# Attention with sinks and a window, then a SwiGLU block: the order of the first groups, the engine of the sink tables, and the path of groups 4 and 5

## The chip, the cores and the metric

The kernel runs on one core of a Trainium2 chip. A core has five engines with a queue of instructions each: TensorE (matrix products; the profile calls it PE, its weight loads PEld), VectorE (DVE), ScalarE (ACT), GpSimd (POOL) and SyncE (SP). Sixteen DMA engines move data between the chip's main memory and the on-chip memory; a transfer is issued from the queue of SyncE, ScalarE or GpSimd, and a transfer that changes float32 to bfloat16 on its way is issued from GpSimd in this kernel. The metric is the time on the device in microseconds (us).

## What is computed

Causal attention over a window of 128 positions plus the first 4 positions as sinks, for 4 batches of 8 heads with 768 positions of 64 elements; the result, as 3072 tokens of 512 elements, goes through a gated block (512 to 1536 to 512). In short:

```python
scores = scale * q @ k.T
keep = (pos_k < 4) | ((pos_q - pos_k >= 0) & (pos_q - pos_k < 128))
a = softmax(where(keep, scores, -1e9))
x = (a @ v) as [batch * position, head * dim]        # 3072 x 512
g = x @ w_gate                                       # 3072 x 1536
out = (g * sigmoid(g) * (x @ w_val)) @ w_out         # 3072 x 512
```

Inputs and outputs are float32; the kernel computes its products in bfloat16 with float32 sums.

## The kernel before

The tokens are split into 12 groups of 256 positions, three to a batch (`g = 3 * b + c`). The steps of a group, by the names of the functions:

- `load_rows` brings keys and queries of a group as bfloat16 rows, `load_nat` does so in token order; `load_v` brings its values.
- `step_T` transposes rows on TensorE, two pairs of heads at a time, and evicts the result from PSUM by ScalarE (keys) or VectorE (queries). `xbar` does the same from the `load_nat` layout by DMA transposes.
- `step_S` makes scores, exponentials (ScalarE) and masks (VectorE, put into `later`).
- `step_K` makes the scores of the sinks for groups that don't start a batch. It needs `ks`, the sink keys of the batch, made by `step_ks` together with `vsb`, the sink values.
- `step_PV` multiplies by the values and normalises; `step_X` transposes the result into `xT`, by TensorE for groups below `XB`, by DMA from there on.
- `gate` is one unit of the gated block (512 columns of gate and of value), `down` one of the output product. Tiles of the block hold `SIZES` tokens; the first three hold 256, then four of 512, then one of 256.

`later` holds VectorE work that is emitted behind the next matmuls; `flush` emits it. Every engine gets its instructions in the order of the program text below.

```python
NROW = 6
XB = 5
FCH = [2, 2, 4, 4]          # the weights of gate and value come in these chunks of 128 columns
...
stp = pool("stp", 2)
...
def load_rows(g, pairs=ALL, tensors=(0, 1)):
    ...
    for i in tensors:
        for w in range(2):
            nc.gpsimd.dma_start(x[64 * w:64 * (w + 1), i, pairs],
                                by_rows((k, q)[i], b, w, pairs, c * 256))
...
# loads at the start
PA, PB = slice(0, 2), slice(2, 4)
new_rows(0)
first = []
for i, eng in ((0, nc.sync), (1, nc.scalar)):
    st = stp.tile([P, 2, 4 * D], FP32, tag="st", name="st")
    for w in range(2):
        eng.dma_start(st[64 * w:64 * (w + 1)], by_rows((k, q)[i], 0, w, PA, 0))
    first.append(st)
nc.gpsimd.iota(tq, ...)
nc.gpsimd.iota(tk, ...)
load_rows(0, PB)
...
load_v(0)
nc.gpsimd.iota(th8, ...)
load_rows(1)
load_gate(0)
load_v(1)
load_gate(1)
load_gate(2)
load_rows(2)
load_v(2)
load_gate(3)
...
def step_T(g, i, p2, evict=None):
    ...
    for pp in range(2):
        p = 2 * p2 + pp
        for r in range(4):
            for w in range(2):
                h = slice(64 * w, 64 * (w + 1))
                nc.tensor.matmul(pt[h, pp, r:256:4], x[h, i, p, r * D:(r + 1) * D],
                                 ident[h, h], ...)
    ...                                    # one eviction, ScalarE or VectorE

def xbar(g):
    ...
    for j in range(2):
        for i in range(2):
            nc.sync.dma_start_transpose((kTs, qTs)[i][b][:, :, t0:t0 + P], nats[g][:, i, j])

def step_ks(b):
    ks = const.tile([P, NP2, KW], BF16, tag=f"ks{b}", name="ks")
    nc.gpsimd.memset(ks, 0.0)
    kss.append(ks)
    for h in range(2):
        r = slice(h * D, (h + 1) * D)
        nc.gpsimd.tensor_copy(out=ks[r, :, h * NS:(h + 1) * NS], in_=kTs[b][r, :, 0:NS])
    vsb = const.tile([P, H, D + 1], BF16, tag=f"vsb{b}", name="vsb")
    nc.gpsimd.tensor_tensor(vsb, vcf[:, b:b + 1].broadcast_to(...), diag_h..., op=ALU.mult)
    vsbs.append(vsb)

def step_K(g):
    ...
    for p in range(NP2):
        nc.tensor.matmul(ps[32 * p:32 * p + KW], kss[b][:, p], qTs[b][:, p, ...], ...)
    es_t[g] = espool.tile([P, 256], BF16, tag="es", name="es")
    nc.scalar.activation(es_t[g], ps, AF.Exp, scale=scale)

def step_X(g, j):
    ...
    if g >= XB:
        ...                                # nc.sync.dma_start_transpose(xTs[tb]..., xns[g, j])
        return
    ...                                    # four transposes by TensorE, one copy by VectorE
...
# the start
warm(10)                                   # ten matmuls on zeros
nc.vector.tensor_copy(out=rows[0][:, 0, PA], in_=first[0])
nc.vector.tensor_copy(out=rows[0][:, 1, PA], in_=first[1])
step_T(0, 0, 0, "a")
step_T(0, 1, 0, "v")
step_S(0, 0)
step_T(0, 0, 1, "v")
step_T(0, 1, 1, "v")
step_S(0, 1)
...
pro(*PVs(0))
flush()
pro(*Xs(0))
flush()
later.append(A(step_ks, 0))
for i in range(4):
    load_out(i)
load_rows(3)
load_v(3)

us = [(alone, 0, 0), g0[0], (alone, 0, 0), g0[1], (alone, 0, 0),
      g1[0], g1[1], g0[2], g1[2], g0[3], g1[3], g0[4], g1[4], g0[5], g1[5],
      *g2, *downs(0), *downs(1), *downs(2)]
weave(us, slots(                           # (unit, attention steps that go into it)
    (0, T(1)), ((1, 2), Ss(1)), (2, [K(1)]), ((3, 3, 4, 4), PVs(1)), (4, Xs(1)),
    ((8, 8, 9, 9), T(2)), ((10, 11), Ss(2)), (11, [K(2)]),
    ((12, 12, 13, 13), PVs(2)), (14, Xs(2)),
    (15, [L(A(load_rows, 4), A(load_v, 4))]),
    ((15, 16, 17, 18), T(3)), ((19, 20), Ss(3)),
    (20, [...loads of groups 5, 6 and 7...]),
    ((21, 21, 22, 22), PVs(3)), (23, Xs(3)),
    ((21, 22, 22, 23), T(4)), ((24, 25), Ss(4)), (25, [K(4)]),
    ((26, 26, 26, 26), PVs(4)), (26, Xs(4))))
...
weave(gates(3) + downs(3), slots(
    (0, [A(xbar, 6)]), (0, [L(A(load_nat, 8), A(load_v, 8))]),
    ((0, 0, 1, 1), T(5)), (4, [A(step_ks, 2)]), *pair(5, 6, 2), ...))
```

`T(g)` of a group that starts a batch also puts `step_ks` of its batch into `later`.

Of the kernel before, what the change touches and what calls it, by code (L numbers as in the profile page):

```python
# [7 lines left out]
FP32 = mybir.dt.float32  # L8
# [6 lines left out]
def kernel(  # L15
# [26 lines left out]
    SIZES = [256, 256, 256, 512, 512, 512, 512, 256]  # L42
    assert sum(SIZES) == NTOK and NG == 12
    OFF = [sum(SIZES[:i]) for i in range(len(SIZES))]
    NROW = 6
    XB = 5

    VS = 72
    FCH = [2, 2, 4, 4]
    FOF = [(i, f - sum(FCH[:i])) for i in range(len(FCH))  # L50
           for f in range(sum(FCH[:i]), sum(FCH[:i + 1]))]
    scale = 1.0 / float(D) ** 0.5
# [1 line left out]
    def pool(name, bufs, psum=False):  # L54
        if psum:
            return ctx.enter_context(
                tc.tile_pool(name=name, bufs=bufs, space=bass.MemoryType.PSUM))
        return ctx.enter_context(tc.tile_pool(name=name, bufs=bufs))
# [2 lines left out]
    wpool = pool("wpool", 1)  # L61
    rowp = pool("rowp", 3)
    natp = pool("natp", 3)
    stp = pool("stp", 2)
    vpool = pool("vpool", 1)
    kqtp = pool("kqtp", 2)
    epool = pool("epool", 2)
# [12 lines left out]
    def bank(shape, dtype, name):  # L80
        return psum.tile(shape, dtype, tag="b", name=name)
# [4 lines left out]
    def by_rows(src, b, w, pairs, t0):  # L86

        hs = slice(2 * pairs.start + w, 2 * pairs.stop, 2)
        return src[b, hs, t0:t0 + 256].rearrange("p (m r) d -> m p (r d)", r=4)
# [7 lines left out]
    def load_rows(g, pairs=ALL, tensors=(0, 1)):  # L97
        b, c = divmod(g, GC)
        x = rows[g] if g in rows else new_rows(g)
        for i in tensors:  # L100
            for w in range(2):
                nc.gpsimd.dma_start(  # L102
                    x[64 * w:64 * (w + 1), i, pairs],
                    by_rows((k, q)[i], b, w, pairs, c * 256))
# [12 lines left out]
    def load_v(g):  # L117
        b, c = divmod(g, GC)
        va = vpool.tile([P, 2, H, VS], BF16, tag=f"va{g}", name="va")
        nc.vector.memset(va[:, :, :, D:D + 1], 1.0)  # L120
        for j in range(2):
            t0 = c * 256 + j * P
            nc.gpsimd.dma_start(  # L123
                va[:, j, :, 0:D], v[b, :, t0:t0 + P].rearrange("h p d -> p h d"))
        vas[g] = va
# [3 lines left out]
    def load_gate(i):  # L129
        f0, n = sum(FCH[:i]) * P, FCH[i] * P  # L130
        for lst, w, nm in ((wgs, moe_w_gate, "wg"), (wvs, moe_w_val, "wv")):
            t = wpool.tile([P, DMC, n], BF16, tag=f"{nm}{i}", name=nm)
            nc.gpsimd.dma_start(
                t, w[:, f0:f0 + n].rearrange("(c p) f -> p c f", p=P))
            lst.append(t)
# [16 lines left out]
    lt8 = const.tile([P, H], FP32)  # L152
    sk = const.tile([P, 1], FP32)
    zero = const.tile([P, 512], BF16)
    vsbs, kss = [], []


    PA, PB = slice(0, 2), slice(2, 4)
    new_rows(0)
    first = []  # L160
    for i, eng in ((0, nc.sync), (1, nc.scalar)):
        st = stp.tile([P, 2, 4 * D], FP32, tag="st", name="st")
        for w in range(2):
            eng.dma_start(st[64 * w:64 * (w + 1)], by_rows((k, q)[i], 0, w, PA, 0))
        first.append(st)
    nc.gpsimd.iota(tq, [[1, P]], base=0, channel_multiplier=0,
                   allow_small_or_imprecise_dtypes=True)
    nc.gpsimd.iota(tk, [[0, 1]], base=0, channel_multiplier=1,
                   allow_small_or_imprecise_dtypes=True)
    load_rows(0, PB)  # L170
    nc.vector.memset(zero, 0.0)
    nc.vector.tensor_scalar(ident, tq, tk, None, op0=ALU.is_equal)
    load_v(0)
    nc.gpsimd.iota(th8, [[-32, NP2], [-NS, 2]], base=0, channel_multiplier=1,
                   allow_small_or_imprecise_dtypes=True)

    load_rows(1)
    load_gate(0)
    load_v(1)
    load_gate(1)  # L180
    load_gate(2)
    load_rows(2)
    load_v(2)
    load_gate(3)

    tq2 = tq.rearrange("p (o x) -> p o x", o=1).broadcast_to([P, 2, P])
    nc.vector.tensor_scalar(mask[:, :, 0:P], tq2, tk, None, op0=ALU.is_lt)
    nc.vector.tensor_scalar(mask[:, :, P:2 * P], tq2, tk, None, op0=ALU.is_ge)
# [2 lines left out]
    nc.vector.tensor_scalar(flat0[:, P:3 * P], flat[:, P:3 * P], sk, None, op0=ALU.max)  # L191
    nc.vector.tensor_copy(out=flat0[:, 3 * P:4 * P], in_=flat[:, 3 * P:4 * P])

    nc.vector.memset(vcf, 0.0)
    for p in range(NP2):
        for w in range(2):
            h = 2 * p + w
# [17 lines left out]
    def step_T(g, i, p2, evict=None):  # L215
        b, c = divmod(g, GC)
        new_T(b)
        x = rows[g]
        pt = bank([P, 2, 256], FP32, "pt")
# [5 lines that stand above are left out]
                    nc.tensor.matmul(  # L225
                        pt[h, pp, r:256:4], x[h, i, p, r * D:(r + 1) * D],
                        ident[h, h], start=True, stop=True, skip_group_check=True)
        dst = (kTs, qTs)[i][b][:, 2 * p2:2 * p2 + 2, c * 256:(c + 1) * 256]
        if (evict or ("a", "v")[i]) == "a":
            nc.scalar.copy(out=dst, in_=pt)  # L230
        else:
            nc.vector.tensor_copy(out=dst, in_=pt)  # L232
# [7 lines left out]
                nc.sync.dma_start_transpose(  # L240
                    (kTs, qTs)[i][b][:, :, t0:t0 + P], nats[g][:, i, j])

    KW = 32

    def step_ks(b):
        ks = const.tile([P, NP2, KW], BF16, tag=f"ks{b}", name="ks")
        nc.gpsimd.memset(ks, 0.0)
        kss.append(ks)
        for h in range(2):
            r = slice(h * D, (h + 1) * D)  # L250
            nc.gpsimd.tensor_copy(  # L251
                out=ks[r, :, h * NS:(h + 1) * NS], in_=kTs[b][r, :, 0:NS])
        vsb = const.tile([P, H, D + 1], BF16, tag=f"vsb{b}", name="vsb")
        nc.gpsimd.tensor_tensor(
            vsb,
            vcf[:, b:b + 1].broadcast_to([P, H, D + 1]),
            diag_h.rearrange("q (h o) -> q h o", o=1).broadcast_to([P, H, D + 1]),
            op=ALU.mult)
        vsbs.append(vsb)
# [32 lines left out]
    def step_K(g):  # L292
        b, c = divmod(g, GC)
        if c == 0:
            return
        ps = bank([P, 256], FP32, "pk")
        for p in range(NP2):
            nc.tensor.matmul(  # L298
                ps[32 * p:32 * p + KW], kss[b][:, p], qTs[b][:, p, c * 256:(c + 1) * 256],
                start=True, stop=True, skip_group_check=True)  # L300
        es_t[g] = espool.tile([P, 256], BF16, tag="es", name="es")
        nc.scalar.activation(es_t[g], ps, AF.Exp, scale=scale)
# [119 lines left out]
    def A(fn, *a):  # L422
        return lambda: fn(*a)

    def T(g):
        b, c = divmod(g, GC)
        def last():
            step_T(g, 1, 1)
            if c == 0:
                later.append(A(step_ks, b))  # L430
        return [A(step_T, g, 0, 0), A(step_T, g, 1, 0), A(step_T, g, 0, 1), last]

    def Ss(g):
        return [A(step_S, g, p2) for p2 in range(2)]
# [27 lines left out]
        return sl  # L462


    def warm(n):
        ps = bank([P, 512], FP32, "w")
        for _ in range(n):
            nc.tensor.matmul(ps, zero[:, 0:P], zero, start=True, stop=True,
                             skip_group_check=True)

    warm(10)
    nc.vector.tensor_copy(out=rows[0][:, 0, PA], in_=first[0])  # L472
    nc.vector.tensor_copy(out=rows[0][:, 1, PA], in_=first[1])
    step_T(0, 0, 0, "a")
    step_T(0, 1, 0, "v")
    step_S(0, 0)
    step_T(0, 0, 1, "v")
    step_T(0, 1, 1, "v")
    step_S(0, 1)

    nc.vector.tensor_scalar(lt8, th8, float(NS), None, op0=ALU.is_lt)
    nc.vector.scalar_tensor_tensor(diag_h, th8, 0.0, lt8, op0=ALU.is_ge, op1=ALU.mult)
    nc.vector.memset(vcf[:, :, D:D + 1], 1.0)
    flush()
    pro(*PVs(0))
    flush()
    pro(*Xs(0))
    flush()
    later.append(A(step_ks, 0))
    for i in range(4):  # L490
        load_out(i)
    load_rows(3)
    load_v(3)

    g0, g1, g2 = gates(0), gates(1), gates(2)
    us = [(alone, 0, 0), g0[0], (alone, 0, 0), g0[1], (alone, 0, 0),
          g1[0], g1[1], g0[2], g1[2], g0[3], g1[3], g0[4], g1[4], g0[5], g1[5],
          *g2, *downs(0), *downs(1), *downs(2)]
    loads = {}

    def L(*fs):
        def f():
            for x in fs:
                x()
        return f

    weave(us, slots(
        (0, T(1)), ((1, 2), Ss(1)), (2, [K(1)]), ((3, 3, 4, 4), PVs(1)), (4, Xs(1)),
        ((8, 8, 9, 9), T(2)), ((10, 11), Ss(2)), (11, [K(2)]),
        ((12, 12, 13, 13), PVs(2)), (14, Xs(2)),  # L510
        (15, [L(A(load_rows, 4), A(load_v, 4))]),
        ((15, 16, 17, 18), T(3)), ((19, 20), Ss(3)),
        (20, [L(A(load_rows, 5), A(load_v, 5), A(load_nat, 6), A(load_v, 6),
                A(load_nat, 7), A(load_v, 7))]),
        ((21, 21, 22, 22), PVs(3)), (23, Xs(3)),
        ((21, 22, 22, 23), T(4)), ((24, 25), Ss(4)), (25, [K(4)]),
        ((26, 26, 26, 26), PVs(4)), (26, Xs(4))))

    def pair(ga, gb, sh=0):
        s = sh  # L520
# [4 lines left out]
                ((14, 14) if s else (13, 14), Xs(gb))]  # L525

    weave(gates(3) + downs(3), slots(
        (0, [A(xbar, 6)]), (0, [L(A(load_nat, 8), A(load_v, 8))]),
        ((0, 0, 1, 1), T(5)), (4, [A(step_ks, 2)]), *pair(5, 6, 2),
        (8, [A(xbar, 7)]), (9, [L(A(load_nat, 9), A(load_v, 9))]),  # L530
        (14, [A(xbar, 8)]), (14, [L(A(load_nat, 10), A(load_v, 10))])))
    weave(gates(4) + downs(4), slots(
# [42 lines left out]
```

## Time and profile before

| | |
|---|---|
| time, median of 3 runs | 284.14 us (283.5 to 286.56) |
| span of the profiled execution | 284.4 us, TensorE's clock 0.934 of full on average |
| TensorE matmuls | 250.3 us busy (88%), 2148 |
| VectorE | 165.4 us (58%), 336 |
| ScalarE | 110.6 us (39%), 213 |
| GpSimd | 73.6 us (26%), 107 |
| chain of work that ended last | TensorE 74%, DMA 9%, GpSimd 5%, VectorE 5% |
| read from main memory, written | 28.34 MB, 6.29 MB |

A line of the profile's tables names the line of the kernel (L298), the engine, and what is written from what (`pk<-qT,ks`). Names of tiles that the text uses: `st` staging tiles of group 0 in float32, `rows` and `nat` keys and queries as loaded, `pt` their transposes in PSUM, `s` and `e` scores and exponentials, `pk` and `es` the same for the sinks, `o` and `xn` attention output, `xT` its transpose, `wg`, `wv`, `wo` the weights, `pg`, `pv`, `pd` their products, `ks` and `vsb` the sink tables, `va` values. In the page's slices each digit stands for a fortieth of the span, 7.11 us, and gives a busy share in tenths.

### The profile page before, as it was taken

Reading aid. Unit: us, or ns where it says so; the run is one execution under the profiler, and the core shown is the slowest. Engines: PE = TensorE matmul, PEld = TensorE weight load, DVE = VectorE, ACT = ScalarE, POOL = GpSimd, SP = SyncE. Lnnn points to the kernel's source line nnn. Section 1 sums busy time; section 2 is a strip of 40 time slices with the busy share of each in tenths; the row PEclk is TensorE's granted clock in tenths of the full one; section 3 lists DMA queues with packets and bytes.
Section 4 is the critical chain, followed back from the end, with each engine's and each line's share of the span. In section 5 each row is a group of like instructions: output and inputs, shape, how many; then the busy total and the mean of one; then the engine's idle time right before and its main releaser. Section 6 shows DMA issues by size and latency. Waiting matters only on the chain.

```text
span 284.4 us, 5371 instructions
## 1 busy us (share of the span) xinstructions
PE 250.3 (88%) x2148; PEld 145.8 (51%) x2174; DVE 165.4 (58%) x336; ACT 110.6 (39%) x213; POOL 73.6 (26%) x107
## 2 busy tenths in 40 slices
PE   6785027999799999999999999978999999999995
PEld 1563015787587545545454454533445544558543
DVE  3566005478857626589851989503899329987400
ACT  1526000237146236474714655123565156233221
POOL 8964465000009990263500080000000000000000
PEclk9659557799999999999999999997999999999999
DMA  8999999100008999399935896157001130010022
GB/s 131 161 191 191 205 203 174 13 0 2 0 3 91 170 179 193 92 111 97 135 52 128 150 103 68 37 128 168 1 20 21 55 129 2 4 36 0 35 79 110
DMA packets 86792, 26.07 MB, mean 92 GB/s; under 512 B 71792, under 2 KB 83824, under 8 KB 86768
## 3 DMA queue, kind: packets, MB, share of 16 engines
q0 software_dynamic: 61760, 13.90, 54.4%
q1 hardware_dynamic: 24720, 11.57, 17.2%
q8 instruction: 17, 0.28, 0.4%
q10 hardware_dynamic: 288, 0.26, 0.3%
q14 instruction: 7, 0.06, 0.1%
HBM read 28.34 MB, written 6.29 MB: 122 GB/s over the span
## 4 chain that ended last, share of the span: by engine, by line
PE 74%; DMA 9%; POOL 5%; DVE 5%; issue 2%; SPq 2%; ACT 2%; POOLq 0%; DVEq 0%
PE pv L374 22%; PE pg L374 21%; PE pd L405 19%; PE o L322 4%; DMA wv<-in_moe_w_val_dram 4%; DMA wo<-in_moe_w_out_dram 4%; PE s L276 3%; PE pt L225 3%; POOL rows L102 2%; SPq L240 2%; DVE ht L388 2%; POOL va L123 2%; DVE xn L328 2%; ACT e L283 1%; DMA xT<-xn 1%
## 5 line engine op out<-in xcount | busy, mean ns | idle before, releaser
L374 PE MATMUL pg<-xT,wg 128*128 128x256 bf16 (+1 forms) x380 | 77.2, 336 | 5.3 <-DMA xT<-xn 2.9
L387 DVE SCALAR_TENSOR_TENSOR u<-th,pg 128x512 bf16<-128x512 f32 x72 | 49.2, 684 | 53.6 <-ACT th L381 53.2
L381 ACT ACTIVATE th<-pg 128x512 f32<-128x512 f32 x72 | 43.4, 603 | 86.4 <-PE pg L374 85.9
L374 PE MATMUL pv<-xT,wv 128*128 128x256 bf16 (+1 forms) x373 | 75.4, 332 | 0.9 <-DVE ht L388 0.5
L405 PE MATMUL pd<-wo,ht 128*128 128x512 bf16 (+1 forms) x289 | 65.7, 370 | 0.6 <-issue 0.2
L388 DVE TENSOR_TENSOR ht<-u,pv 128x512 bf16<-128x512 bf16 x72 | 49.5, 688 | 13.7 <-PE pv L374 6.9
L374 PEld LDWEIGHTS <-wg 128*128 128x128 bf16 x384 | 38.3, 101 | 32.3 <-DMA xT<-xn 3.1
L283 ACT ACTIVATE e<-s 128x512 bf16<-128x512 f32 (+1 forms) x96 | 46.0, 576 | 4.3 <-PE s L276 4.2
L374 PEld LDWEIGHTS <-wv 128*128 128x128 bf16 x384 | 34.9, 100 | 21.9 <-issue 3.2
L405 PEld LDWEIGHTS <-ht 128*128 128x128 bf16 x300 | 27.5, 98 | 27.2 <-issue 0.3
L409 ACT ACTIVATE ot<-pd 128x512 f32<-128x512 f32 (+1 forms) x25 | 14.5, 582 | 49.2 <-PE pd L405 43.9
L288 DVE TENSOR_TENSOR e<-e,mask 128x1024 bf16<-128x1024 bf16 (+1 forms) x48 | 29.1, 641 | 5.4 <-ACT e L283 5.2
L123 POOL DMA_DIRECT2D va<-in_v_dram x24 | 21.8, 936 | 3.7 <-issue 2.1
L322 PEld LDWEIGHTS <-e 128*128 128x128 bf16 x352 | 17.9, 102 | 7.8 <-DVE e L288 1.5
L328 DVE TENSOR_TENSOR xn<-o,rcp 128x256 bf16<-128x256 f32 x48 | 20.4, 424 | 1.7
L251 POOL COPY ks<-kT 64x16 bf16<-64x16 bf16 x8 | 1.6, 194 | 73.9 <-ACT kT L230 37.7
L322 PE MATMUL o<-va,e 128*128 128x65 bf16 x352 | 19.7, 200 | 0.7 <-DVE e L288 0.7
L225 PE MATMUL pt<-ident,rows 64*64 64x64 bf16 x384 | 16.0, 268 | 1.4 <-DVE rows L472 1.4
L225 PEld LDWEIGHTS <-rows 64*64 64x64 bf16 x384 | 13.4, 147 | 6.6 <-issue 4.1
L298 PE MATMUL pk<-qT,ks 128*32 128x256 bf16 x32 | 2.5, 297 | 16.0 <-POOL ks L251 16.0
L276 PE MATMUL s<-qT,kT 64*128 64x128 bf16 (+1 forms) x256 | 14.8, 248 | 1.6 <-DVE qT L232 1.6
L232 DVE CAST qT<-pt 128x512 bf16<-128x512 f32 x12 | 8.3, 692 | 10.5 <-PE pt L225 10.5
(44 smaller groups left out, 117.6 us busy)
## 6 DMA issues: line engine op xcount, KB each, us to landing
out_dram<-ot SPq DMA_DIRECT2D x23, 256.0 KB
va<-in_v_dram POOLq DMA_DIRECT2D x24, 128.0 KB, 6.1
wo<-in_moe_w_out_dram POOLq DMA_DIRECT2D x4, 384.0 KB, 12.2
nat<-in_k_dram POOLq DMA_DIRECT2D x12, 128.0 KB, 4.6
nat<-in_q_dram POOLq DMA_DIRECT2D x12, 128.0 KB, 5.3
rows<-in_k_dram POOLq DMA_DIRECT2D x10, 128.0 KB, 5.7
rows<-in_q_dram POOLq DMA_DIRECT2D x10, 128.0 KB, 5.5
wg<-in_moe_w_gate_dram POOLq DMA_DIRECT2D x2, 512.0 KB, 9.7
```

Of the source, the lines that this page charges most:

```text
L123: nc.gpsimd.dma_start(va[:, j, :, 0:D], v[b, :, t0:t0 + P].rearrange("h p d -> p h d"))
L225: nc.tensor.matmul(pt[h, pp, r:256:4], x[h, i, p, r * D:(r + 1) * D], ident[h, h], start=True, stop=True, skip_group_check=True)
L276: nc.tensor.matmul(pss[2 * pp + h][:, col:col + n], kTs[b][r, p, kk:kk + P], qTs[b][r, p, qq:qq + n], start=True, stop=True)
L283: nc.scalar.activation(e_t[g][:, h0 + h, lo:512], pss[2 * pp + h][:, lo:512], AF.Exp, scale=scale)
L288: nc.vector.tensor_tensor(e, e, m[:, :, lo:512].broadcast_to([P, 2, 512 - lo]), op=ALU.mult)
L322: nc.tensor.matmul(o, l, r, start=(i == 0), stop=(i == len(mms) - 1), skip_group_check=True)
L328: nc.vector.tensor_tensor(xns[g, j][:, 256 * hh:256 * (hh + 1)].rearrange("p (h d) -> p h d", h=4), po[:, :, 0:D], rcp.broadcast_to([P, 4, ...
L374: nc.tensor.matmul(ps[:, i * n:(i + 1) * n], ws[fi][:, c, fo * P:(fo + 1) * P], x[:, c], start=(c == 0), stop=(c == DMC - 1))
L381: nc.scalar.activation(th, pg, AF.Tanh, scale=0.5)
L387: nc.vector.scalar_tensor_tensor(u, th, 1.0, pg, op0=ALU.add, op1=ALU.mult)
L388: nc.vector.tensor_tensor(hts[tb][:, f:f + two].rearrange("p a n -> p (a n)"), u, pv, op=ALU.mult)
L405: nc.tensor.matmul(po, hts[tb][:, f, ts * P:(ts + 1) * P], wos[f // n][:, f % n, lo:hi], start=(f == 0), stop=(f == DFC - 1))
```

## The change

Four things are changed.

- **Group 0 pair by pair.** Keys and queries of the first two pairs of heads come in one float32 transfer each and are cast by VectorE and ScalarE; the other two pairs come by casting transfers from GpSimd's queue. Each pair is transposed, scored and masked by itself, with a few matmuls on zeros between, so that work can start when the first pair is there.
- **Group 1 earlier.** Its rows are the first thing loaded after group 0, and it is transposed and half scored before the values of group 0 are multiplied. The weights of gate and value come in five chunks instead of four, and the output weights are loaded ahead of the rows of group 3 in the starting block.
- **Sink tables by VectorE.** The copies of the sink keys and the product for the sink values leave GpSimd, whose queue also issues the loads. The key tables of all batches are one tile, cleared once at the start.
- **Groups 4 and 5 by the DMA crossbar.** Their keys and queries are loaded in token order and transposed by DMA, which the kernel does for the later groups already; with `XB = 4` so is the attention output of group 4. The steps of groups 1 to 6 move to other units accordingly.

```diff
-    XB = 5
+    XB = 4
-    FCH = [2, 2, 4, 4]
+    FCH = [2, 2, 2, 2, 4]
-    stp = pool("stp", 2)
+    stp = pool("stp", 4)
@@ loads at the start
-    for i, eng in ((0, nc.sync), (1, nc.scalar)):
-        st = stp.tile([P, 2, 4 * D], FP32, tag="st", name="st")
-        for w in range(2):
-            eng.dma_start(st[64 * w:64 * (w + 1)], by_rows((k, q)[i], 0, w, PA, 0))
-        first.append(st)
+    first = {}
+    for p in range(2):
+        for i, eng in ((0, nc.sync), (1, nc.scalar)):
+            st = stp.tile([P, 4 * D], FP32, tag="st", name="st")
+            eng.dma_start(st, by_pair((k, q)[i], p))
+            first[p, i] = st
+    nc.scalar.activation(warmed, one, AF.Exp)
+    pair_by_cast(2, 0)
     nc.gpsimd.iota(tq, ...)
     nc.gpsimd.iota(tk, ...)
-    load_rows(0, PB)
+    pair_by_cast(2, 1)
+    pair_by_cast(3, 0)
+    pair_by_cast(3, 1)
+    load_rows(1)
     load_v(0)
+    load_gate(0)
+    load_v(1)
     nc.gpsimd.iota(th8, ...)
-    load_rows(1)
-    load_gate(0)
-    load_v(1)
     load_gate(1)
     load_gate(2)
+    load_gate(3)
     load_rows(2)
     load_v(2)
-    load_gate(3)
+    load_gate(4)
+    for i in range(4):
+        load_out(i)
@@ step_ks
-        nc.gpsimd.memset(ks, 0.0)
-            nc.gpsimd.tensor_copy(
-                out=ks[r, :, h * NS:(h + 1) * NS], in_=kTs[b][r, :, 0:NS])
-        nc.gpsimd.tensor_tensor(
+            nc.vector.tensor_copy(
+                out=kss[r, b, :, h * NS:(h + 1) * NS], in_=kTs[b][r, :, 0:NS])
+        nc.vector.tensor_tensor(
             vsb, ...
@@ the start
-    warm(10)
-    ...
+    fill(8, bank([P, 512], FP32, "w"))
+    for p in range(2):
+        nc.vector.tensor_copy(out=rows[0][:, 0, p], in_=first[p, 0])
+        nc.scalar.copy(out=rows[0][:, 1, p], in_=first[p, 1])
+        pair_T(p, "a")
+    pair_S(0, 1)
+    pair_T(2, "v")
+    pair_S(1)
+    pair_mask(0)
+    pair_T(3, "v")
+    pair_S(2, 1)
+    pair_mask(1)
+    pair_S(3, 1)
+    pair_mask(2)
+    step_T(1, 0, 0, "a")
+    pair_mask(3)
+    step_T(1, 1, 0, "v")
+    step_T(1, 0, 1, "a")
+    step_T(1, 1, 1, "v")
+    step_S(1, 0)
+    masks1 = list(later)
+    later.clear()
+    step_PV(0, 0, 0)
+    step_PV(0, 0, 1)
+    flush()
+    step_PV(0, 1, 0)
+    step_PV(0, 1, 1)
+    step_X(0, 0)
+    flush()
+    step_S(1, 1)
+    step_X(0, 1)
+    ...
+    for m in masks1[:2]:
+        m()
+    step_ks(0)
+    for m in masks1[2:]:
+        m()
+    step_K(1)
     load_rows(3)
     load_v(3)
@@ the first units
-    us = [(alone, 0, 0), g0[0], (alone, 0, 0), g0[1], (alone, 0, 0),
-          g1[0], g1[1], g0[2], ...
+    us = [g0[0], (alone, 0, 0), g0[1], g1[0], g1[1], g0[2], ...
-        (0, T(1)), ((1, 2), Ss(1)), (2, [K(1)]), ((3, 3, 4, 4), PVs(1)), (4, Xs(1)),
-        ((8, 8, 9, 9), T(2)), ((10, 11), Ss(2)), (11, [K(2)]),
-        ((12, 12, 13, 13), PVs(2)), (14, Xs(2)),
-        (15, [L(A(load_rows, 4), A(load_v, 4))]),
-        ((15, 16, 17, 18), T(3)), ((19, 20), Ss(3)),
-        ...
-        ((21, 22, 22, 23), T(4)), ((24, 25), Ss(4)), (25, [K(4)]),
-        ((26, 26, 26, 26), PVs(4)), (26, Xs(4))))
+        (1, PVs(1) + Xs(1)),
+        ((5, 5, 6, 6), T(2)), ((7, 8), Ss(2)), (8, [K(2)]),
+        ((9, 9, 10, 10), PVs(2)), (11, Xs(2)),
+        (12, [...load_nat and load_v of groups 4, 5 and 6...]),
+        ((13, 14, 15, 16), T(3)), ((17, 18), Ss(3)), (18, [A(step_ks, 1)]),
+        (18, [A(xbar, 4)]),
+        ((19, 19, 20, 20), PVs(3)), (21, Xs(3)),
+        ((20, 21), Ss(4)), (21, [K(4)]), (22, [A(xbar, 5)]),
+        ((22, 22, 23, 23), PVs(4)), (23, Xs(4))))
@@ the first tile of 512 tokens
-        (0, [A(xbar, 6)]), (0, [L(A(load_nat, 8), A(load_v, 8))]),
-        ((0, 0, 1, 1), T(5)), (4, [A(step_ks, 2)]), *pair(5, 6, 2),
+        (0, [L(A(load_nat, 7), A(load_v, 7))]), (2, [A(xbar, 6)]),
+        (2, [L(A(load_nat, 8), A(load_v, 8))]), (5, [A(step_ks, 2)]), *pair(5, 6),
```

## The prediction

> **What bounds the kernel now.** I read four views in this order: the page's 40 slices (7.11 us each), the stretches of time around what they show, the chain of work that ended last, and the waits of TensorE. The slices first:
>
> ```profile
> PE   6785027999799999999999999978999999999995
> PEclk9659557799999999999999999997999999999999
> DMA  8999999100008999399935896157001130010022
> ```
>
> From slice 7 on TensorE is busy nine tenths at full clock, so most of the kernel is bound by TensorE. The exception is the front: slices 4 and 5 (28 to 43 us) are nearly empty, and the clock is at half before and after. By stretches (length, then busy us of each engine, clock, DMA share):
>
> ```profile
> core 0: us, PE busy (x) PEld busy (x) DVE busy (x) ACT busy (x) POOL busy (x), PEclk, DMA share, GB/s
> 0.00:25.00 25.00, 19.43 (x226) 12.82 (x226) 12.83 (x38) 8.36 (x17) 18.77 (x32) 0.73 1.30 167
> 25.00:41.00 16.00, 0.01 (x2) 0.01 (x3) 2.76 (x5) 2.48 (x6) 8.67 (x14) 0.64 1.39 199
> 41.00:53.40 12.40, 10.49 (x81) 7.43 (x82) 4.88 (x13) 1.58 (x3) 5.54 (x8) 0.64 1.32 131
> 53.40:284.40 231.00, 220.33 (x1843) 125.51 (x1867) 144.89 (x281) 98.18 (x189) 40.61 (x53) 0.99 0.58 74
> ```
>
> So 16.0 us pass with no matmul, 12.4 us follow at a clock of 0.64, and 231.0 us are nearly full. The waits of TensorE between 20 and 60 us name one cause, and the chain (start, duration, what) says what stood before it:
>
> ```profile
> PE pk L298 <- POOL ks L251: 16.0, 1, 16.0
> ```
>
> ```profile
> 13.78 11.86 DMA wv<-in_moe_w_val_dram
> ...
> 26.65 10.52 DMA wo<-in_moe_w_out_dram
> ...
> 38.18 0.91 POOL va L123
> ...
> 40.22 0.22 POOL ks L247
> ...
> 40.99 0.40 PE pk L298 x3
> 41.40 1.82 PE pg L374 x8
> ```
>
> TensorE wants the sink keys `ks` of batch 0 for the sink scores of group 1. GpSimd makes them, but only behind the loads that it issues earlier in program order: the output weights, the rows of group 3, the values of group 3. It holds at most eight loads open (the load issued at 16.33 starts right after the eighth before it landed, at 16.05), so its queue moves at the pace of the DMA, which is full until about 50 us. The two copies take 0.43 us; 16 us is the queue. The weights are no reason: the trace's completions put gate/value chunk 0 at 14.2 and 16.1 us, chunk 1 at 19.1 and 20.4, the last value weights at 35.2, the last output weights at 42.8.
>
> **What the skill says.** (1) "TensorE: Matmul & The Clock Gate", section "Part 1: The HAM clock gate", says that the array runs at half clock after an idle window of about 3.4 us and at full clock only after a sustained busy one. The trace agrees: eight 256-column matmuls take 1.86 us at 50 us and advance every 0.87 us from 53.5 us. (2) The same page, section "Architectural detail", says that VectorE, ScalarE and GpSimd are strictly first in, first out. The 16 us behind loads show that for GpSimd, and it means that table work put on VectorE makes everything behind it wait for its inputs. (3) "GPSIMD Engine Reference", section "Performance versus the Vector engine", measures a two-input elementwise operation 1.96 times slower on GpSimd. Here the `vsb` product (128x520) takes 1.06 us on GpSimd; with that ratio my estimate for VectorE is 0.54 us, no run of this kernel shows it.
>
> **The change part by part.**
>
> *Sink tables.* Two copies and one product leave GpSimd for VectorE, four times. At 2 x 0.2 for the copies (what they take on GpSimd) plus 0.54, that is 0.9 us a batch, 3.8 us in all. VectorE is busy 144.9 of 231 us in the long stretch, so three of the four are hidden. The first is in the front, and the wait of 16.0 us goes.
>
> *The front.* I lay it out anew. The first K and Q pair now comes in one transfer each. Before, all four staging transfers had landed at 6.55, after about 0.72 MB since 2.1 us; the first pair is half of the staging data, so about 4.5 us. Then:
> - pair casts to about 5.0, four pairs of transposes (16 matmuls; 32 took 1.08 to 1.92), scores, evictions and filler: about 1.7 us a pair at half clock, to about 11.5 us;
> - transposes of group 1: its rows land by about 10 us (same bytes ahead of them as before, when they landed at 12.3), 64 matmuls took 3.6 us cold: about 14.5;
> - scores of half of group 1 (0.62 to 0.8): 15.3; values of group 0 (4 steps): about 17, the values having landed near 12;
> - four normalisations on VectorE (0.18 + 0.42 each, 2.4 us), their transposes and two 0.42 copies, with the other half of the scores beneath: about 19.6;
> - VectorE: two tiny table operations (0.35), two masks (2 x 0.69), the key copies (2 x 0.2): about 21.7. Here the sink scores of group 1 wait some 2 us, in place of the 16;
> - first gate unit, two groups of eight matmuls at 0.87 us: 23.5. Values and normalisation of group 1, which VectorE sets (two masks 1.3, the unit's two products 1.4, normalisation 2.4, copies), to about 27.6; then two units of 1.74: 31.1 us.
>
> This is the point that the old kernel reaches at 53.4. Part of this comes from the old 41 to 53 us, which ran mostly cold. I add 1.4 us for cold windows in mine: **32.5**, a gain of **20.9 us** (18 to 23). Can the weights keep up? Bytes and order up to each chunk are nearly as before, so chunk 2 lands near 23, chunk 3 near 26, chunk 4 at 35.2. Chunk 4 is first read after five more units (8.7), the transposes (2.2) and half the scores of group 2: 44 us. The output weights (42.8) are needed past 65. All of it is in time.
>
> *Groups 4 and 5 by the crossbar.* These lines of TensorE's timeline (start, busy, operation) price what goes:
>
> ```profile
> 77.72 1.05 PE L374 MATMUL pg<-xT,wg 128*128 128x256 bf16 x8 [1.45 <-DVE xT L354]
> 94.38 0.63 PE L225 MATMUL pt<-ident,rows 64*64 64x64 bf16 x16
> 94.95 1.25 PE L405 MATMUL pd<-wo,ht 128*128 128x512 bf16 x5
> 116.11 1.08 PE L225 MATMUL pt<-ident,rows 64*64 64x64 bf16 x32
> 117.12 1.04 PE L374 MATMUL pv<-xT,wv 128*128 128x512 bf16 x3
> ```
>
> One transposing step holds TensorE for 0.57 us (94.38 to 94.95), two for 1.01 (116.11 to 117.12). Group 4: 4 x 0.57 = 2.3; group 5: 2 x 1.01 = 2.0; together **4.3 us**, all on the path, since TensorE has no idle there. Transposing the attention output of group 4 by DMA as well saves 2 x 0.22 = **0.4 us** (113.58 to 113.80). VectorE and ScalarE lose four evictions each of about 0.6, hidden. The DMA does it behind: the row loads of groups 4 to 6 are no longer held behind the tables on GpSimd's queue, so they can be on the chip long before; a DMA transpose holds its queue 1.2 us.
>
> *Reordering.* Group 2 finishes a unit earlier, so the wait of 1.45 us for its transposed output (first line above) should vanish: **-1.4 us**.
>
> *A new wait.* Group 4's output transposes stand behind group 5's four key/query transposes on one queue (4 x 1.3 = 5.2 us). These start about 0.9 us into the fourth of the six `down` units (2.6 to 3.5 us each), once the third's output is copied. The last output transpose then issues at about +7.8 us and lands 2.45 later (as the one before 193.28): +10.3, while TensorE gets there at +9.6. **+1.0 us** with some margin.
>
> Sum: 20.9 + 4.3 + 0.4 + 1.4 - 1.0 = 26.0. 284.1 - 26.0 = **258 us**.
>
> **The rivals.**
> 1. *The DMA takes the place of the tables.* For it: the DMA is saturated for the first 50 us, and the chain shows 11.86 and 10.52 us of weight loads. Against it: those are links only because GpSimd's queue ran through them; the completions are ahead of the need by 5 to 20 us. If an early unit did wait for weights, I lose 3 to 6 us: about 263.
> 2. *VectorE takes the place of GpSimd.* Tables on a strict queue: if batch 2's keys come late (four transposes issued three units before they are read), VectorE stops and TensorE after it. For: the margin is some 3 us by the queue count above. Against: in the old run the DMA queue ran well ahead of TensorE (the keys of group 9 were transposed from 158.3, their unit starts near 172). Cost if so 2 to 5 us: 260 to 263.
> 3. *The front stays cold and serial.* Pair by pair, each piece is a short chain TensorE, ScalarE/VectorE, TensorE. If no window fills, everything to the third unit runs at half clock: 36 instead of 32.5, and 261 to 262.
> 4. *The gain is hidden*: the time freed in front is lost again later. Against: after 53.4 TensorE is 95% busy (220.3 of 231.0), and nothing there waits for a fixed clock time. The one later wait of size, at 190 us (2.87 us for a transposed output, then a half-clock window), stays as it is.
>
> **Range and chances.** The front is worth 18 to 23, the crossbar 3 to 6, new waits 0 to 5. That gives 252 to 265. The 16 us wait has one clear cause, and the change moves its work away, so a gain under 2% (5.7 us) would need two rivals together: faster 0.96, same 0.02, slower 0.02.
>
> **What would show it.** Right: no wait of TensorE for `ks` over 3 us; first gate unit near 22 and the fourth near 32 us; the empty slices gone and clock 1.0 from about slice 4; no transposes by TensorE for groups 4 and 5; a wait of about 1 us for a transposed output where the 512-token tiles begin. Wrong: waits of early units for `wg` or `wv`; VectorE idle on transposed keys; a half-clock stretch past 30 us; a new wait over 3 us at the first 512-token tile.

## The result and the profile after

The changed kernel takes 273.8 us (median of 4 runs, 272.8 to 274.6) where the kernel before takes 285.4 in the same runs: a ratio of 0.960, 95% interval 0.952 to 0.968. The prediction was 258 us, with a range from 252 to 265. The direction was right, the size was not: 26 us were expected, and 11.6 came.

The slices of the page of the changed kernel (6.79 us each) show where to look:

```profile
PE   5039679999999958999999999969999999999995
PEclk9999999999999997999999999988999999999999
DMA  3949999999995379999149910462010320000122
```

The two empty slices at 28 to 43 us are gone. In their place slice 1 is empty and slice 2 three tenths busy, between 6.8 and 20 us, and the DMA, which used to be full from slice 0 on, is now weak in slices 0 and 2. Slices 14 and 15 (95 to 109 us) are thinner than before. The stretches around these places (length, busy us of each engine, clock, DMA share):

```profile
core 0: us, PE busy (x) PEld busy (x) DVE busy (x) ACT busy (x) POOL busy (x), PEclk, DMA share, GB/s
0.00:13.10 13.10, 3.60 (x8) 1.04 (x8) 3.03 (x15) 1.89 (x3) 6.37 (x14) 1.00 0.65 82
13.10:18.50 5.40, 1.08 (x18) 0.84 (x18) 0.72 (x2) 0.78 (x2) 0.92 (x1) 1.00 0.46 58
18.50:41.90 23.40, 19.03 (x283) 13.83 (x284) 17.32 (x46) 11.17 (x23) 17.79 (x25) 1.00 1.44 163
41.90:98.90 57.00, 55.76 (x622) 39.64 (x624) 40.20 (x83) 25.41 (x50) 25.84 (x31) 1.00 1.56 149
98.90:106.20 7.30, 3.34 (x18) 1.32 (x19) 0.69 (x1) 2.04 (x4) 4.45 (x6) 0.77 1.51 168
```

The clock of 1.00 in the first rows is not what the matmuls show. The trace has no entry of the clock before 24.3 us, and until then sixteen transposing matmuls take 1.06 us, while from 24.6 us on sixty-four take 1.97:

```profile
13.12 1.06 PE L486 MATMUL pt<-ident,rows 64*64 64x64 bf16 x16 [8.30 <-DVE rows L517]
24.65 1.97 PE L244 MATMUL pt<-ident,rows 64*64 64x64 bf16 x64
```

So TensorE ran at half clock up to there. In the first 13.1 us it does nothing but its 3.6 us of filler. DMA moves 82 and then 58 GB/s, where the kernel before had 167 GB/s over its first 25 us. The longest waits of TensorE in the changed kernel (waited for: us in total, times, longest) give the causes their names:

```profile
PE pt L486 <- DVE rows L517: 12.6, 2, 8.3
PE pg L388 <- DMA xT<-xn: 6.5, 2, 4.0
PE pk L312 <- DVE kss L265: 2.3, 1, 2.3
```

The 16.0 us for the sink keys have become 2.3. New are 12.6 us for the first two pairs of group 0, and 6.5 us for transposed outputs, of which the 4.0 at 98.9 us are new and the 2.5 at 178 us were there before (2.9 at 190 us). The front of the chain of work, with start and duration, says what the first of these is:

```profile
0.74 0.71 SPq L175
1.51 16.60 DMA st<-in_k_dram
18.14 0.30 DVE rows L517
18.48 1.06 PE pt L486 x9
```

The staging transfer of the second key pair, issued at 1.51, is read at 18.1 us. It brings 128 KB.

### The profile page after: what moved, and what is told of

It is laid out like the page before. It is cut to its first block, busy times and chain, and to the rows that moved or that the text cites. A ratio compares the mean times of both kernels' runs of the same rounds, so it can differ in the third digit from the quotient of the medians.

```text
span 271.5 us, 5112 instructions
## 1 busy us (share of the span) xinstructions
PE 240.5 (89%) x2016; PEld 138.4 (51%) x2039; DVE 165.6 (61%) x347; ACT 109.8 (40%) x213; POOL 71.1 (26%) x93
## 4 chain that ended last, share of the span: by engine, by line
PE 74%; DVE 9%; DMA 9%; SPq 3%; ACT 3%; issue 2%; DVEq 0%; ACTq 0%
PE pv L388 22%; PE pg L388 21%; PE pd L419 19%; DMA st<-in_k_dram 6%; PE o L336 4%; PE s L290 4%; DMA xT<-xn 2%; DVE ht L402 2%; DVE xn L342 2%; SPq L259 2%; PE pt L244 2%; ACT e L297 1%; DVE e L302 1%; DVE u L401 1%; PE pt L486 1%
## 5 line engine op out<-in xcount | busy, mean ns | idle before, releaser
L388 PE MATMUL pg<-xT,wg 128*128 128x256 bf16 (+1 forms) x380 | 75.3, 329 | 6.7 <-DMA xT<-xn 6.5
L388 PE MATMUL pv<-xT,wv 128*128 128x256 bf16 (+1 forms) x374 | 74.9, 328 | 1.4 <-DVE ht L402 0.8
L388 PEld LDWEIGHTS <-wg 128*128 128x128 bf16 x384 | 37.6, 99 | 33.0 <-issue 6.1
L388 PEld LDWEIGHTS <-wv 128*128 128x128 bf16 x384 | 34.5, 98 | 21.5 <-issue 4.0
L297 ACT ACTIVATE e<-s 128x512 bf16<-128x512 f32 (+1 forms) x88 | 42.9, 580 | 3.6 <-PE s L290 3.5
L111 POOL DMA_DIRECT2D nat<-in_k_dram x16 | 14.2, 903 | 55.5 <-DMA qT<-nat 50.9
L302 DVE TENSOR_TENSOR e<-e,mask 128x1024 bf16<-128x1024 bf16 (+1 forms) x44 | 26.9, 649 | 2.9 <-ACT e L297 2.9
L336 PEld LDWEIGHTS <-e 128*128 128x128 bf16 x352 | 16.5, 98 | 6.3 <-issue 0.2
L336 PE MATMUL o<-va,e 128*128 128x65 bf16 x352 | 17.8, 193 | 0.0
L486 PE MATMUL pt<-ident,rows 64*64 64x64 bf16 x64 | 4.2, 341 | 12.6 <-DVE rows L517 12.6
L111 POOL DMA_DIRECT2D nat<-in_q_dram x16 | 14.3, 919 | 0.0
L341 DVE RECIPROCAL rcp<-o 128x4 f32<-128x4 f32 x48 | 8.5, 177 | 6.9 <-PE o L336 6.7
L290 PEld LDWEIGHTS <-kT 64*128 64x128 bf16 x240 | 8.1, 97 | 7.8 <-issue 7.1
## 6 DMA issues: line engine op xcount, KB each, us to landing
wo<-in_moe_w_out_dram POOLq DMA_DIRECT2D x4, 384.0 KB, 11.6
```

The lines of the kernel that those rows point to most:

```text
L111: nc.gpsimd.dma_start(x[:, i, j].rearrange("p (h d) -> p h d", d=D), src[b, :, t0:t0 + P].rearrange("h p d -> p h d"))
L290: nc.tensor.matmul(pss[2 * pp + h][:, col:col + n], kTs[b][r, p, kk:kk + P], qTs[b][r, p, qq:qq + n], start=True, stop=True)
L297: nc.scalar.activation(e_t[g][:, h0 + h, lo:512], pss[2 * pp + h][:, lo:512], AF.Exp, scale=scale)
L302: nc.vector.tensor_tensor(e, e, m[:, :, lo:512].broadcast_to([P, 2, 512 - lo]), op=ALU.mult)
L336: nc.tensor.matmul(o, l, r, start=(i == 0), stop=(i == len(mms) - 1), skip_group_check=True)
L388: nc.tensor.matmul(ps[:, i * n:(i + 1) * n], ws[fi][:, c, fo * P:(fo + 1) * P], x[:, c], start=(c == 0), stop=(c == DMC - 1))
```

## The experiments

Two theories stood after this. *Staging*: the new transfers over a pair of heads are slow by their form. *Queue*: the wait at 98.9 us is SyncE's queue, in which group 5's transposes stand ahead of group 4's outputs. The times of the runs, each beside the kernel before on the same chip:

| run | median, us | ratio to before, 95% interval |
|---|---|---|
| the change | 273.8 | 0.960 (0.952 to 0.968) |
| e1: all first transfers over 64 rows | 264.7 | 0.924 (0.916 to 0.932) |
| e2: the staging transfers alone | 265.3 | 0.929 (0.924 to 0.935) |
| e3: the casting transfers alone | 276.0 | 0.966 (0.960 to 0.971) |
| e4: group 5's transposes early | 267.2 | 0.937 (0.931 to 0.944) |
| e5: before, tables by VectorE alone | 269.2 | 0.943 (0.937 to 0.950) |
| e6: four buffers for `nat` | 272.9 | 0.954 (0.949 to 0.959) |
| e7: all repairs | 253.4 | 0.887 (0.881 to 0.892) |
| e8: SyncE's order alone, both places | 263.7 | 0.924 (0.919 to 0.929) |
| e9: group 8's loads held back | 272.6 | 0.953 (0.947 to 0.959) |
| e10: e8, groups 4 and 5 by TensorE | 269.4 | 0.945 (0.940 to 0.949) |

The ratio of e1 leaves out its slowest execution, 1.5% above its fastest, which is also the one profiled.

**e1, the first transfers over 64 rows.**

```diff
-            eng.dma_start(st, by_pair((k, q)[i], p))
+            for w in range(2):
+                eng.dma_start(st[64 * w:64 * (w + 1)],
+                    (k, q)[i][0, 2 * p + w, 0:256].rearrange("(m r) d -> m (r d)", r=4))
...
-        nc.gpsimd.dma_start(rows[0][:, i, p], by_pair((k, q)[i], p))
+        w = p - 2
+        nc.gpsimd.dma_start(rows[0][64 * w:64 * (w + 1), i, 2:4],
+                            by_rows((k, q)[i], 0, w, slice(2, 4), 0))
```

> The changed kernel, with the first transfers of group 0 written so that the slowest dimension of each source is 64 rows instead of 2 heads: each staging transfer is cut into one per head, and the four casting transfers each bring one head of two pairs. Same bytes; four more issues on the SyncE and ScalarE queues. Theory (a transfer over 2 heads is spread over 2 DMA engines, so the first pair lands at 12.8 and 18.1 us and the casts, at 15.4 to 19.8 us, hold GpSimd's eight open loads): first pair there by about 6 us, pair transposes start by about 7, fourth gate unit at about 33 us instead of 41.9, time 273.8 - 9 = about 265 us. Rival (descriptors are starved by VectorE's early work, or the early DMA is slow for another reason): no change, 273 to 274 us.

Measured 264.7 us. The same bytes in twice as many transfers. These lines are of VectorE's timeline, first of the changed kernel, then of e1:

```profile
12.78 0.29 DVE L517 CAST rows<-st 128x256 bf16<-128x256 f32 x1 [8.46 <-DMA st<-in_k_dram]
18.14 0.29 DVE L517 CAST rows<-st 128x256 bf16<-128x256 f32 x1 [3.08 <-DMA st<-in_k_dram]
```

```profile
4.78 0.29 DVE L523 CAST rows<-st 128x256 bf16<-128x256 f32 x1 [0.94 <-DMA st<-in_k_dram]
6.98 0.70 DVE L523 CAST rows<-st 128x256 bf16<-128x256 f32 x1
```

The first pair is cast 8 us earlier, the second 11 us earlier. The fourth gate unit begins at 32.7 us (41.9 in the changed kernel). The reason can be counted. Queue q10 is ScalarE's; it carries nothing but the staged queries. Its line in the page's table of queues (packets, MB, share), of the kernel before, of the changed one and of e1:

```profile
q10 hardware_dynamic: 288, 0.26, 0.3%
```

```profile
q10 hardware_dynamic: 260, 0.26, 0.3%
```

```profile
q10 hardware_dynamic: 320, 0.26, 0.4%
```

In all three, 256 packets are data of 1024 bytes. The rest, by the trace, are packets of 4 bytes: 32 for two transfers before, 4 for two after the change, 64 for four in e1. That is 16, 2 and 16 a transfer. The Trainium skill explains what these count: "DMA: Bandwidth & Descriptors", section "Why a DMA increments its semaphore by 16 and not by 1", says that of a transfer issued from SyncE or ScalarE only the engines that take part post an increment each, and that their number is the largest up to 16 that divides the slowest dimension of size over 1 of both sides. For the pair transfer that dimension of the source is the two heads, so by this rule two of sixteen engines carry it; for one head it is 64 rows, so all sixteen do. The counts agree with it. The number of transfers is not the reason: the kernel before had four of 128 KB as well, each over 64 rows, and by the trace's completions all had landed by 6.5 us.

**e2 and e3, one kind of transfer at a time.** e2 has the first hunk above alone, e3 the second alone.

> The changed kernel, with only the four float32 staging transfers cut into one per head; the casting transfers of pairs 2 and 3 stay over two heads. Theory (both kinds are slow for the same reason): the first two pairs are there by 6 us, but the casts still land near 14 us or later and hold back values and weights, so half of the gain: about 269 us. If the staging alone matters: about 265 us, as with all cut. If the casts alone matter: 273 to 274 us.

> The changed kernel, with only the four casting transfers of pairs 2 and 3 rewritten (each one head of two pairs, 64 rows as slowest dimension); the float32 staging transfers stay over two heads. Theory (the staging transfers, squeezed through two DMA engines, hold the start, and every other transfer also has a share on those two engines): the first pair still lands near 12.8 and the second near 18, and the rows of group 1 still near 20 us; 272 to 274 us. Rival (the casts hold GpSimd's eight open loads and are half of the cause): about 269 us.

e2 measured 265.3 us, which cannot be told from e1. The expected half was wrong: with the staging repaired the casts, still over two heads, land between 7.8 and 11.0 us by the trace, late enough to be seen but not in the way, since the pairs before them keep TensorE busy. e3 measured 276.0, no gain: its second key pair is cast at 19.7 us. So the form of the staging is the cause of all that e1 gained, within the noise. A transfer on two engines also slows the others: in e3 the casts, on sixteen, land at 7.8 to 11.2 us, and the rows of group 1 at 13.4 to 19.2, against 9.3 to 11.8 in e1. The completions show how: of the sixteen of the first of these transfers of rows in e3, fourteen came between 6.95 and 7.43 us and the last two at 13.41 and 13.42. That these two shares lie on the engines that carry the staging is an inference; the trace doesn't name the engine of a packet.

**e4 and e8, SyncE's order.**

```diff
-        (18, [A(xbar, 4)]),
+        (18, [A(xbar, 4), A(xbar, 5)]),
...
-        ((20, 21), Ss(4)), (21, [K(4)]), (22, [A(xbar, 5)]),
+        ((20, 21), Ss(4)), (21, [K(4)]),
...                                       # e8 has this as well, in the second tile of 512 tokens
-        (9, [L(A(load_nat, 11), A(load_v, 11))]), (13, [A(xbar, 10)])))
+        (9, [L(A(load_nat, 11), A(load_v, 11))]), (15, [A(xbar, 10)])))
```

> The changed kernel, with the crossbar transposes of group 5 issued right behind those of group 4 instead of four units later, just ahead of group 4's output transposes on the same queue. Theory (the 4.0 us wait for a transposed output at 98.9 us is the queue of SyncE, and it costs a half-clock window as well): the wait goes below 1 us, 4 to 5.5 us faster, 268.5 to 270 us. Rival (the output transpose is late because the DMA itself is busy with loads): the wait stays at 3 us or more, 273 us.

> The changed kernel with the order of SyncE's queue alone repaired, in both places: transposes of group 5 earlier, those of group 10 later. Theory: both waits for a transposed output are under 0.5 us, no half-clock window after 40 us, 2.5 us below the 267.2 us of the run with group 5 alone: about 264.5 us. Rival (the wait at 178 us is set by the landing of the output transpose itself): it stays above 2 us, 267 us.

e4 measured 267.2 us, 6.6 below the change, a little more than expected. Its waits list has only the old one, `PE pg L388 <- DMA xT<-xn` of 2.5 us at 172.6. e8 measured 263.7 and has none. No half-clock window is left in either after 40 us. So both waits came from the queue's order. The kernel before has the transposes of group 10 in the same place, so its wait at 190 us has most likely the same cause; that was not run.

**e6 and e9, is part of the wait a collision?** In the changed kernel the last output transpose is issued at 98.45 and TensorE goes on at 102.86:

```profile
97.13 2.56 SPq L360 DMA_TRANSPOSE xT<-xn  x2
98.09 1.76 POOL L111 DMA_DIRECT2D nat<-in_k_dram  x2 [19.60 <-DMA qT<-nat]
102.86 1.87 PE L388 MATMUL pg<-xT,wg 128*128 128x512 bf16 x4 [4.00 <-DMA xT<-xn]
```

The middle line is the loads of group 8. They were waiting for the buffer that group 5's transposes had just freed, and start between the two output transposes. e6 gives `nat` four buffers (`natp = pool("natp", 4)`). e9 holds these loads until the output is there:

```diff
+    held = const.tile([P, 1], BF16)
+    def hold():
+        nc.gpsimd.tensor_copy(out=held, in_=xTs[3][:, 0, 511:512])
...
-        (2, [L(A(load_nat, 8), A(load_v, 8))]), (5, ...
+        (2, [hold, L(A(load_nat, 8), A(load_v, 8))]), (5, ...
```

> The changed kernel with four buffers instead of three for the rows in token order; everything else as it is, the crossbar transposes of group 5 still ahead of group 4's output transposes on SyncE's queue. Theory A (part of the 4.0 us wait is a collision: the late transposes of group 5 free the buffer for the loads of group 8, which then start at 98.1 us, just when the output transposes are under way, so these land 4.4 us after issue instead of 2.45): the wait falls to about 2 us, 271 to 272 us. Theory B (the queue alone): the wait stays at 4 us, 273.5 us.

> The changed kernel, with one tiny GpSimd copy that reads the last of group 4's transposed output ahead of the loads of group 8: these can no longer start while the output transposes are under way. Group 5's crossbar transposes stay where they are. Theory A (collision is part of the 4.0 us wait): the last output transpose lands about 2.3 us after its issue, as in the run with group 5 early, instead of 4.3, and the wait falls to 2.0 us; 271 to 272 us. Theory B (queue alone): the landing stays above 4 us and the wait at 4 us, 273.5 us.

e6 measured 272.9 us and a wait of 3.4, and doesn't tell the two apart: with one more buffer the loads of group 9 start at 98.6, in the same place and for the same reason.

```profile
102.48 1.02 PE L388 MATMUL pg<-xT,wg 128*128 128x512 bf16 x4 [3.36 <-DMA xT<-xn]
```

e9 does. Its timeline in the same stretch:

```profile
98.64 2.53 SPq L360 DMA_TRANSPOSE xT<-xn  x2
102.52 1.43 PE L388 MATMUL pg<-xT,wg 128*128 128x512 bf16 x4 [2.16 <-DMA xT<-xn]
103.04 1.76 POOL L111 DMA_DIRECT2D nat<-in_k_dram  x2 [0.41 <-issue]
```

The last output transpose lands 2.4 us after its issue instead of 4.3, and the wait is 2.2 us: about half of it was the collision. In the time this is 1.2 us (272.6), and the interval overlaps that of the change. The length of the wait alone does not say whether a window at half clock follows: the traces have one of 3.4 us after the waits of 4.0 (the change) and 2.2 us (e9), and none after those of 3.4 (e6) and 2.5 us (e4).

**e5, the tables alone in the kernel before.**

```diff
-        ks = const.tile([P, NP2, KW], BF16, tag=f"ks{b}", name="ks")
-        nc.gpsimd.memset(ks, 0.0)
-        kss.append(ks)
...
-            nc.gpsimd.tensor_copy(out=ks[r, :, h * NS:(h + 1) * NS], ...
+            nc.vector.tensor_copy(out=kss[r, b, :, h * NS:(h + 1) * NS], ...
...
-        nc.gpsimd.tensor_tensor(vsb, ...
+        nc.vector.tensor_tensor(vsb, ...
```

> The kernel before with one part of the change alone: sink tables by VectorE, key tables in one tile cleared at the start. Theory (GpSimd's queue, not the weights, held TensorE for 16 us, and the cold 12 us after it went with it): the wait for the key tables falls below 2 us, 16 to 20 us faster, 265 to 269 us, so this part alone does more than the whole change. Rival (the weights would have held TensorE next): a new wait for wg or wv of several us in the first 40 us, 275 us or more.

269.2 us, 15.9 below before, at the edge of what was expected. None of TensorE's waits is for tables or weights:

```profile
PE pg L372 <- DMA xT<-xn: 2.9, 1, 2.9
PE px L349 <- DVE xn L326: 2.7, 5, 0.8
PE pg L372 <- DVE xT L352: 2.0, 2, 1.4
PE o L320 <- ACT es L300: 2.0, 2, 1.6
```

This one part brings more than the whole change.

**e10, groups 4 and 5 back on TensorE.** From e8:

```diff
-        (12, [L(A(load_nat, 4), A(load_v, 4), A(load_nat, 5), A(load_v, 5),
+        (12, [L(A(load_rows, 4), A(load_v, 4), A(load_rows, 5), A(load_v, 5),
...
-        (18, [A(xbar, 4), A(xbar, 5)]),
+        ((17, 18, 18, 19), T(4)), ((20, 21, 22, 22), T(5)),
```

> The changed kernel with SyncE's order repaired in both places (the 263.7 us run), and groups 4 and 5 loaded in rows and transposed by TensorE again, eight steps of 16 matmuls in the units before their scores; nothing else. Theory (the steps lie on the path at 0.5 to 0.57 us each): 4.0 to 4.6 us slower, about 268 us. Rival (TensorE has slack there, or the crossbar costs as much as it saves): within 1 us of 263.7.

269.4 us, 5.7 above e8 and more than expected. The two profiles differ by 1.7 us before the fourth gate unit, where nothing was changed (the half-clock windows there sum to 23.9 us in e10 and 17.1 in e8), and by 5.3 us after it. The crossbar's part is real; why it is 1 us more than planned is not shown.

**e7, all repairs:** e1, e8, and the key tables ahead of the masks.

```diff
-    for m in masks1[:2]:
-        m()
     step_ks(0)
-    for m in masks1[2:]:
+    for m in masks1:
         m()
```

> The changed kernel with all repairs: transfers of group 0 over 64 rows, transposes of group 5 right behind those of group 4, transposes of group 10 behind instead of ahead of group 8's output transposes, key tables of batch 0 ahead of the masks on VectorE. Theory: 273.8 - 9 (staging) - 6.6 (group 5) - 2.5 to 4.2 (group 10, with or without a half-clock window) - 1.5 (tables first) = about 253 to 255 us, faster than both kernels and than every run so far. Rival (the savings overlap, or the freed DMA time collides elsewhere): 258 us or more.

253.4 us, faster than both kernels, and what the sum said. The wait for the tables fell from 2.3 us to 1.1; what this part brings was not run alone. The busy times and slices of its page (6.25 us each):

```profile
PE 238.8 (96%) x2039; PEld 137.7 (55%) x2039; DVE 165.5 (66%) x347; ACT 109.5 (44%) x213; POOL 70.1 (28%) x93
PE   7788899899999999999999999999999999999994
PEclk9797999999999999999999999999999999999999
```

## Why the prediction was wrong

The prediction's sum was 20.9 us from the front, 6.1 from the crossbar and the reordering, less 1.0 for a new wait: 26.0. The two profiles (284.4 and 271.5) differ by 12.9. The missing 13.1 us lie in two steps, which divide at the start of the fourth gate unit. (A unit fills 512 columns of PSUM; for a tile of 256 tokens these are 256 columns of gate and of value.) Three units and the attention of groups 0 and 1 are done by then in all of these kernels: the one before, the changed one and e1.

```profile
53.36 1.04 PE L374 MATMUL pg<-xT,wg 128*128 128x256 bf16 x8
41.92 1.04 PE L388 MATMUL pg<-xT,wg 128*128 128x256 bf16 x8
32.67 1.04 PE L394 MATMUL pg<-xT,wg 128*128 128x256 bf16 x8
```

**The front: 9.4 us missing.** The fourth unit begins at 41.9 us, not at 32.5 (53.4 before: a gain of 11.5, not 20.9). The step that failed is "The first K and Q pair now comes in one transfer each", with its "about 4.5 us". I worked it out from the bytes and took the rate of the old transfers for the new form. The diff shows a source whose slowest dimension is two heads; the prediction did not ask what that form costs. With the form repaired, e1 reaches the fourth unit at 32.7 us, and waits 2.3 us for the tables where the prediction had "some 2 us". The other steps of the front were right in sum, although single ones were off: the pairs took until 14.0 us instead of 11.5, and group 1's transposes 2.0 us at full clock instead of 3.6 at half. e1 also ran at half clock from 20.7 to 27.5 us, where the plan had 1.4 us for all such windows. That the sum is met within 0.2 us is in part luck.

**The tables** were right. GpSimd's queue, not the weights, was the 16 us (e5), and no run shows TensorE waiting for `wg`, `wv` or `wo`. One term was mis-sized without harm: the product takes 0.70 us on VectorE, not 0.54, since GpSimd is only 1.5 times slower here and not the 1.96 that "GPSIMD Engine Reference", section "Performance versus the Vector engine", has for 2048 elements; the measurement decides. The eight open loads, too, need a word: in the trace GpSimd's loads take eight semaphores in turn, and each waits for the load that used its semaphore before. So the limit is one of this program; no run shows whether the hardware has one.

**After the front: 3.7 us missing.** From the fourth unit to the end the time went from 231.0 to 229.6 us, where the prediction had 225.9. The step that failed is "A new wait", "+1.0 us": the mechanism was named and only its size was off. It measured 4.0 us, by two terms. Group 5's transposes started 1.8 us into their `down` unit, not 0.9, which put the last output transpose 1.2 us later. And it landed 4.3 us after issue instead of 2.45, because of loads that the prediction did not see: group 5's late transposes are what frees their buffer (e9). A third term was left out, though the prediction had cited the clock gate: the trace of the changed kernel has a half-clock window behind this wait, 3.4 us from 102.8 on, which costs up to half of that. (The other window after 40 us, at 181.3, has its like in the kernel before, at 193.3.) 3.0 and up to 1.7 us are more than the 3.7 that are missing; that the crossbar gave about 1 us more than planned (e10) would make up for the rest.

**The crossbar and the reordering** were right. The 1.45 us wait for group 2's output is gone from the list of waits. The transposes of groups 4 and 5 were put at 4.3 us; e10 against e8 gives 5.7 by the medians and 5.3 by the profiles.

**The rivals.** None of the four was the cause. DMA did become the bound at the start, but by the form of four small transfers and not by the weights, as the first rival had it. The second (VectorE held by late keys) is not in the trace, which has no wait of VectorE for transposed keys. The third (a cold front) holds only up to 24.3 us, where the pairs run at half clock; the plan had them so, and what made them late was their transfers. The fourth (the gain is lost later) isn't it either: after the fourth unit the time fell by 1.4 us. Of the prediction's own signs of being wrong two came: a wait over 3 us at the first tile of 512 tokens and a half-clock stretch past 30 us. The range does not follow from its own terms: with the 1.4 us of the reordering they give 254 to 267 us, not 252 to 265. It had room for 5 us of new waits, and none for a transfer that takes three times as long.

## What to carry to other kernels

Read the shape of a transfer before its bytes: a source whose slowest dimension is 2 was carried by two DMA engines, took 8 to 17 us for 128 KB, and slowed what ran beside it. Count the small completion packets of a queue if in doubt; that worked here on the queues of SyncE and ScalarE, but not for GpSimd's casting transfers, where the changed kernel has 3779 packets of 4 bytes in the first 26 us, and e1 346. When work moves to a DMA queue, write down what stands ahead of it and what its end releases; two sets of transposes moved in program order were worth 10 us here (e8), more than the 5.7 us that the crossbar saved for groups 4 and 5 (e10). And try the parts of a change alone: the smallest one here brought more than the whole.

## What was not expected of the hardware

- A pair transfer of 128 KB posts two completion packets instead of sixteen, and four of them, 0.52 MB, needed until about 18 us, some 33 GB/s; the same bytes were there by 6.5 us over sixteen engines.
- A DMA transpose of a 128x512 tile landed 2.3 to 2.4 us after issue with no loads beside it, and 4.3 with the first of six loads issued 0.4 us before it.
- The key copies and the product of the sink tables took 0.18 and 0.70 us on VectorE, 0.19 and 1.06 on GpSimd: the copies gain nothing by the move itself, only by the queue.
